# Loading the last second-layer pieces by column halves, and storing left halves of the output behind them

## The chip, the cores and the metric

The kernel runs on one core of a Trainium2 chip. The metric is device time in microseconds (us), median of three runs. The core has a matrix engine (TensorE, PE in the profile), three engines for elementwise work (VectorE, ScalarE, GpSimd: DVE, ACT, POOL) and a sync engine (SyncE, SP) whose queue issues every transfer between main memory and the on-chip memory here. Transfers run on 16 DMA engines. A transfer is cut into packets: one packet for each contiguous run of bytes.

## The reference

An attention over 8 batches, 8 heads, 576 positions gives a matrix `x` of 4608 rows and 512 columns. A soft mixture of experts follows, and only its end matters here:

```python
slot_input = (d.T @ x).reshape(E, S_per_e, D)     # 8 experts, 4 slots each, 512 wide
for e in range(E):
    h = np.maximum(slot_input[e] @ w1[e], 0.0)    # 512 -> 1024
    slot_out[e] = h @ w2[e]                       # 1024 -> 512
...
return (c @ slot_out)                             # 4608 x 32 times 32 x 512
```

`c` is a softmax over the 32 slots of every row's logits. Every row of the output needs all 32 rows of `slot_out`, and a column of the output needs only that column of `slot_out`. All values are 32 bits wide.

## The kernel before

The attention part works through four pairs of batches. While it runs, the weights of the experts are already being loaded: `w1` and `w2` are 16 MB each, and a load moves a piece of 1 MB. A pool of such slots (`ws`) lies over buffers of the attention part as they come free.

**First layer.** For each expert two pieces of `w1` are multiplied with the slot inputs (`expert_in`, L1332); 32 rows by 256 columns leave at a time, four such tiles side by side. A ReLU and a transpose give `hT`, the hidden values with hidden units on partitions.

**Second layer.** `expert_out` (L1366) loads each `w2[e]` in two pieces. A piece holds 512 hidden units as 128 partitions with twice two rows of 512 columns. `mult` makes four matmuls for each column half: the left 256 columns gather in the bank `kvbank`, the right 256 in `scbank` (`pacc[0]` and `pacc[1]`), over all 16 pieces. The sums stand as four stacks of 32 partitions, to be added at the end. The last of the 16 pieces is loaded in four quarter-size transfers, left columns first.

**Weights of the rows.** `slots(bp)` makes `c` for one of four row blocks (`L` holds the logits, 128 partitions with 9 rows each), splits each value into a rounded part and a rest, and transposes it into `cT`.

**The end.** `slot_sums` (L1303) copies each accumulator to `accs` and adds the four stacks with one matmul by the constant `rep` (L1316) into `so`; `sr` holds the sum as a rounded part (L1499) and a rest (L1504). `out_mult` (L1513) makes one row block of 128 by 512 of the output in a bank, from `cT` and `sr`; ACT or DVE copies it to an output buffer (L1566, L1568); three such blocks go to main memory in one transfer of 768 KB (L1576), in runs of 6 KB for each partition. The first three blocks are made in column halves and stored one by one, in runs of 2 KB (L1546).

**What sets the order.** A planner (`Plan.order`) writes the whole order of every engine's instructions ahead, from costs that the code gives for each step and from a model of the DMA engines (`DMA_RATE` and so on). The program then runs each engine's list in order; an instruction waits for what it needs, and what stands behind it waits too. The SP queue is such a list as well. A transfer also waits until the eighth transfer before it has landed, since eight completion semaphores are used in turn.

Of the kernel before, what the change touches and what calls it, by code (L numbers as in the profile page):

```python
# [17 lines left out]
FILL = 10 ** 6  # L18


class Plan:
# [57 lines left out]
    def order(self):  # L79
# [13 lines left out]
        while ready:  # L93
# [44 lines left out]
            if dma:  # L138
                start = max(t, dma_free)
                dma_free = start + dma  # L140
                end[i] = dma_free + self.DMA_LAG
                free[eng] = start
            else:
                end[i] = free[eng] = t + cost
# [124 lines left out]
def kernel(  # L269
# [226 lines left out]
    DMA_RATE = 412e3  # L496
    IN_RATE = 386e3

    def load(dst, src, nbytes, w, pri=None):
        add(  # L500
            SP, 0.06, lambda: nc.sync.dma_start(dst(), src), w=[w],  # L501
            dma=nbytes / (DMA_RATE if nbytes in (1 << 20, 1 << 18) else IN_RATE), pri=pri,
        )
# [738 lines left out]
    NOUT, G = 6, 3  # L1242
# [20 lines left out]
    )  # L1263
    late_tiles = []

    def late(x, off, n):
        if not late_tiles:
# [3 lines left out]
            late_tiles.append(pool.tile([P, J * HALF + JN + DM], F32, name="cS"))  # L1271
        return late_tiles[x][:, off: off + n]

    def after_q(x, off, n, count=1):
# [6 lines left out]
    css, cxs, acs = (  # L1281
        after_q(1, 0, J * HALF), after_q(1, J * HALF, JN), after_q(1, J * HALF + JN, DM)
# [5 lines left out]
    EG = 4  # L1288
    hTb = hTs.tile().split(E // EG)
# [12 lines left out]
    so = [b_l.tile(), b_m.tile()]  # L1302

    def slot_sums():
        for d in range(2):
# [7 lines left out]
            )  # L1313
            add(
# [8 lines left out]
    def expert_in(e, hb):  # L1323
        w1v = w1[e].rearrange("(c p) f -> p c f", p=P)
        w1b = [load_w(w1v[:, 2 * i: 2 * i + 2], wqs if e == EG else ws) for i in range(2)]
        for i in range(2):

            def f(i=i):
                wv = w1b[i].ap.rearrange("p (c f) -> p c f", c=2)
                for c in range(2):  # L1330
                    for j in range(4):
# [3 lines left out]
                            wv[:, c, 256 * j: 256 * j + 256],  # L1335
# [33 lines left out]

    def expert_out(e):  # L1370
        w2v = w2[e].rearrange("(j p t) d -> p j (t d)", j=4, t=2)
        w2h = w2[e].rearrange("(j p t) d -> p j t d", j=4, t=2)
        for i in range(2):
            last = e == E - 1 and i == 1
            t = ws.tile()
            wide = lambda t=t: t.ap.rearrange("p (j t d) -> p j t d", j=2, t=2)

            def mult(dst, d0, n, start, stop, i=i, wide=wide):
                for t in range(2):
                    for j in range(2):  # L1380

                        x = 2 * t + j
                        nc.tensor.matmul(  # L1383
                            dst[NS * x: NS * x + NS, :n],
                            hT()[:, 4 * t + 2 * i + j, NS * e: NS * e + NS],
                            wide()[:, j, t, d0: d0 + n],
                            start=start,
                            stop=stop,
                            tile_position=(0, NS * x),
                        )  # L1390

            if not last:
                load(
                    lambda t=t: t.ap.rearrange("p (a x) -> p a x", a=2),
                    w2v[:, 2 * i: 2 * i + 2], 1 << 20, t,
                )
                for d in range(2):
                    add(
                        PE, (0.5, 16),
                        lambda d=d, mult=mult, i=i: mult(  # L1400
                            pacc[d].ap[:, 0], d * HD, HD, e == 0 and i == 0, False
                        ),
                        r=[hTb.part(e // EG), t], w=[pacc[d]],
                    )
                continue
            t.split(4)
            for d in range(2):
                for j in range(2):
                    load(
                        lambda d=d, j=j: wide()[:, j, :, d * HD: d * HD + HD],  # L1410
                        w2h[:, 2 * i + j, :, d * HD: d * HD + HD], 1 << 18, t.part(2 * d + j),
                    )
            for d in range(2):
                add(
                    PE, (0.5, 16), lambda d=d, mult=mult: mult(pacc[d].ap[:, 0], d * HD, HD, False, True),
                    r=[hTb.part(e // EG), t.part(2 * d), t.part(2 * d + 1)], w=[pacc[d]],
                )

# [3 lines left out]
    cT = {}  # L1422

    def slots(bp):
        Lb = L[bp]
        lv = Lb.ap.rearrange("p (j n) -> p j n", j=J)
        mx, sm, cxb, csb = cmxs.tile(), csms.tile(), cxs.tile(), css.tile()
        cx = lambda: cxb.ap.rearrange("p (j n) -> p j n", n=NS)
# [8 lines left out]
            r=[Lb, mx], w=[cxb],  # L1437
# [9 lines left out]
        add(DVE, 1.2, f, r=[cxb], w=[sm, cxb])  # L1447

# [9 lines left out]
        for t, js in enumerate((range(0, 6, 2), range(6, J, 2))):  # L1458
# [9 lines left out]
            add(PE, len(js) * 0.14, f, r=[csb, ident_b], w=[tp], also=[ct])  # L1468
# [19 lines left out]
    for e in range(E):  # L1488
        expert_out(e)
        if e < NBP:  # L1490
            slots(e)


    slot_sums()
    outv = out.rearrange("(p j) d -> p j d", j=J)
# [26 lines left out]
    ot0 = ots.tile().split(2 * G)  # L1522
    for d in range(2):
        x = slice(d * HD, d * HD + HD)
        for i in range(G):
            po = b_o.tile()
            add(
                PE, 0.22, lambda po=po, i=i, x=x: out_mult(0, i, po, x),
                r=[sr.part(d), cT[0]], w=[po], also=[ot0],
            )  # L1530

            def f(po=po, i=i, d=d):
                dst = ot0.ap[:, i * DM + d * HD: i * DM + d * HD + HD]
                if d == 0 or i == 1:
                    nc.scalar.copy(dst, po.ap[:, :HD])
                else:
                    nc.vector.tensor_copy(dst, po.ap[:, :HD])

            add(
                *((ACT, act(HD)) if d == 0 or i == 1 else (DVE, dve(HD))), f,  # L1540
                r=[po], w=[ot0.part(2 * i + d)],
            )
            if d == 1:
                add(
                    SP, 0.06,
                    lambda i=i: nc.sync.dma_start(  # L1546
# [66 lines left out]
```

## Time and profile before

| | before |
|---|---|
| median of 3 runs | 207.63 us (207.09 to 207.95) |
| profiled execution, its own time | 207.2 us |
| its span, first to last instruction | 205.4 us |
| moved by DMA | 76.47 MB in 28986 packets, 372 GB/s over the span |
| read from main memory, written to it | 66.65 MB, 9.44 MB |
| busy: PE, DVE, POOL, ACT | 82%, 65%, 41%, 34% |

The page of the profile gives busy shares in 40 slices of 5.1 us, the chain of work that ended last, and groups of instructions. Other views give the instructions in order of time, who waited for whom, and, for chosen stretches of the span, the busy time of each engine with the clock that TensorE was granted (1.00 is full), the mean busy share of the 16 DMA engines, and GB/s. That share counts the time of packets, which overlap a little, so that a full stretch reads 1.02 to 1.06.

### The profile page before, as it was taken

To read this page: it belongs to the slowest core of one execution; us is meant where nothing else is said; L and a number is where in the kernel's file an instruction comes from. 1 tells how busy PE (TensorE), PEld (TensorE's weight loads), DVE (VectorE), ACT (ScalarE), POOL (GpSimd) and SP (SyncE) were. 2 spreads that over 40 slices of the span, in tenths; PEclk is the share of its full clock that TensorE was granted. 3 is DMA by queue.
4 is the path that set the end of the run, shared out by engine and by line. 5 is a ranking of instruction groups with operands and counts; after the bars stand their busy time and mean duration, and the time that the engine had idled before them with its cause. 6 is when DMAs were issued, how large, how long until landed. Compare 5 with 4: busy or idle time off the path is not lost.

```text
span 205.4 us, 5935 instructions
## 1 busy us (share of the span) xinstructions
PE 167.9 (82%) x2565; PEld 106.1 (52%) x2565; DVE 133.3 (65%) x232; ACT 69.8 (34%) x183; POOL 84.2 (41%) x84
## 2 busy tenths in 40 slices
PE   7999649978699899788999787989999957989400
PEld 6677534635366586455576364656555523545100
DVE  7822540899897999999899984672558400486500
ACT  2022405446541846436453430200113300475300
POOL 7199205689992995799834482000000000000000
PEclk9999996999979999999999999999999997899755
DMA  6999999999999999999999999999999995099994
GB/s 204 365 393 392 382 388 383 388 385 383 395 384 388 381 391 390 388 394 401 406 400 412 406 413 408 407 409 407 410 405 406 410 395 183 0 396 409 415 420 201
DMA packets 28986, 76.47 MB, mean 372 GB/s; under 512 B 1824, under 2 KB 6944, under 8 KB 28960
## 3 DMA queue, kind: packets, MB, share of 16 engines
q1 hardware_dynamic: 28960, 76.09, 96.9%
q8 instruction: 20, 0.33, 0.7%
q14 instruction: 6, 0.05, 0.1%
HBM read 66.65 MB, written 9.44 MB: 370 GB/s over the span
## 4 chain that ended last, share of the span: by engine, by line
PE 37%; DMA 21%; DVE 14%; POOL 11%; issue 4%; SPq 4%; ACT 2%; POOLq 1%; DVEq 1%; ACTq 0%
DMA arena<-in_moe_w_dram 9%; DMA arena<-in_v_dram 8%; PE bank L1332 7%; PE scbank L812 6%; PE kvbank L703 4%; PE bank L881 4%; SPq L501 4%; DMA out_dram<-arena 4%; POOL arena L847 3%; POOL arena L668 3%; PE bank L1513 3%; POOL arena L647 3%; POOL arena L870 2%; PE bank L1009 2%; DVE arena L605 2%
## 5 line engine op out<-in xcount | busy, mean ns | idle before, releaser
L647 POOL TENSOR_TENSOR arena<-arena 128x1152 f32<-128x1152 f32 x8 | 21.0, 2632 | 17.4 <-ACT arena L640 14.9
L590 DVE STREAM_TRANSPOSE arena<-top 128x1152 f32<-128x1152 f32 x16 | 21.6, 1353 | 8.2 <-DMA top<-in_q_dram 8.2
L703 PE MATMUL kvbank<-arena 64*32 64x128 f32 x1152 | 21.0, 277 | 6.2 <-issue 2.7
L812 PE MATMUL scbank<-arena 64*64 64x288 f32 x256 | 23.7, 447 | 2.3 <-DVE arena L826 2.3
L519 PE MATMUL kvbank<-ones 128*128 128x256 f32 x82 | 23.4, 422 | 2.4 <-ACT arena L727 1.3
L668 POOL TENSOR_TENSOR arena<-arena 128x128 f32<-128x128 f32 (+2 forms) x32 | 23.4, 730 | 3.2 <-ACT arena L656 1.3
L870 POOL TENSOR_TENSOR arena<-arena,ssm 128x576 f32<-128x576 f32 x16 | 18.3, 1151 | 9.6 <-DVE ssm L866 7.9
L703 PEld LDWEIGHTS kvbank<-arena 64*32 64x32 f32 x1152 | 16.5, 107 | 10.8 <-issue 5.6
L847 POOL TENSOR_TENSOR arena<-arena,smx 128x576 f32<-128x576 f32 x16 | 18.4, 1150 | 7.7 <-DVE smx L842 7.7
L881 PE MATMUL bank<-arena 128*128 128x288 f32 x64 | 18.7, 425 | 1.3 <-DVE arena L873 0.8
L605 DVE TENSOR_REDUCE arena<-arena 128x128 f32<-128x1152 f32 x8 | 17.2, 2155 | 3.9 <-DMA arena<-in_phi_dram 3.7
L519 PEld LDWEIGHTS kvbank<-ones 128*128 128x128 f32 x82 | 15.8, 207 | 6.0 <-ACT arena L727 1.7
L1513 PE MATMUL bank<-sr,cT 64*128 64x512 f32 (+1 forms) x78 | 14.7, 425 | 1.7 <-DVE arena L1568 1.3
L826 DVE STREAM_TRANSPOSE arena<-scbank 128x576 f32<-128x576 f32 x16 | 12.3, 766 | 5.6 <-PE scbank L812 5.5
L812 PEld LDWEIGHTS scbank<-arena 64*64 64x64 f32 x256 | 9.9, 141 | 10.2 <-DVE arena L826 3.7
L852 ACT ACTIVATE arena<-arena 128x576 f32<-128x576 f32 x16 | 10.9, 684 | 11.3 <-POOL arena L847 11.1
L881 PEld LDWEIGHTS bank<-arena 128*128 128x128 f32 x64 | 11.2, 189 | 6.4 <-DVE arena L873 2.1
L1383 PE MATMUL kvbank<-arena 128*32 128x256 f32 x128 | 10.8, 411 | 3.8 <-DMA arena<-in_moe_w_dram 3.8
L1568 DVE COPY arena<-bank 128x512 f32<-128x512 f32 x17 | 11.1, 688 | 4.2 <-PE bank L1513 2.5
L873 DVE STREAM_TRANSPOSE arena<-arena 128x576 f32<-128x576 f32 x16 | 11.9, 755 | 1.5 <-POOL arena L870 1.5
L1332 PE MATMUL bank<-arena,SIM 128*32 128x256 f32 x224 | 12.5, 379 | 0.4 <-DVE SIM L1232 0.4
L857 DVE TENSOR_REDUCE ssm<-arena 128x18 f32<-128x576 f32 x16 | 11.8, 738 | 1.0 <-ACT arena L852 0.7
(130 smaller groups left out, 238.4 us busy)
## 6 DMA issues: line engine op xcount, KB each, us to landing
arena<-in_moe_w_dram SPq DMA_DIRECT2D x29, 1024.0 KB, 15.3
top<-in_q_dram SPq DMA_DIRECT2D x8, 1152.0 KB, 12.6
arena<-in_k_dram SPq DMA_DIRECT2D x8, 1152.0 KB, 10.1
arena<-in_v_dram SPq DMA_DIRECT2D x8, 1152.0 KB, 12.5
out_dram<-arena SPq DMA_DIRECT2D x11, 768.0 KB, 8.7
arena<-in_phi_dram SPq DMA_DIRECT2D x8, 576.0 KB, 7.1
top<-in_moe_w_dram SPq DMA_DIRECT2D x2, 1024.0 KB, 11.1
arena<-in_moe_w_dram SPq DMA_DIRECT2D x4, 256.0 KB, 14.6
```

Source lines behind the costliest of these rows:

```text
L519: lambda: nc.tensor.matmul(warm.ap, ones, ones.unsqueeze(1).to_broadcast([P, 2, P]), start=True, stop=True,),
L590: lambda: nc.vector.transpose(qT.ap.rearrange("p (i u y) -> p u i y", i=2, y=Y), qt.ap[:, h * QT_SZ: h * QT_SZ + QT_SZ].rearrange("p (u i ...
L605: lambda: nc.vector.tensor_reduce(mx.ap[:, c0:c1], ph().rearrange("p c j m -> p c m j"), axis=AX.X, op=ALU.max),
L647: lambda: nc.gpsimd.tensor_tensor(ph(), ph(), mb.ap[:, c0:c1].unsqueeze(2).to_broadcast([P, c1 - c0, J, M]), op=ALU.subtract,),
L668: plus = lambda o, x, y: nc.gpsimd.tensor_tensor(o, x, y, op=ALU.add)
L703: nc.tensor.matmul(acc.ap[M * c: M * c + M, a, : 2 * D], ph()[h0: h0 + HALF, c, j, :], kv()[h0: h0 + HALF, :, c, j * D: j * D + D], start= ...
L812: nc.tensor.matmul(scb.ap[HALF * g: HALF * g + HALF, a, :JY], pair[g].kd.ap[h0: h0 + HALF, i, c].rearrange("p r m -> p (r m)"), pair[g].qT ...
L847: lambda: nc.gpsimd.tensor_tensor(exv(), exv(), bc(mx), op=ALU.subtract),
L870: lambda: nc.gpsimd.tensor_tensor(exv(), exv(), bc(sm), op=ALU.mult),
L881: nc.tensor.matmul(lp.ap[:, :JY], vpb.ap[:, h, :], aT.ap[:, a * JY: (a + 1) * JY], start=(h == 0), stop=(h == H - 1),)
L1332: nc.tensor.matmul(hb.ap[NS * j: NS * j + NS, :256], SIM.ap[:, 2 * i + c, NS * e: NS * e + NS], wv[:, c, 256 * j: 256 * j + 256], start=(e ...
L1513: nc.tensor.matmul(po.ap[:, : x.stop - x.start], cT[bp].ap[y: y + HALF, j // 2 * P: j // 2 * P + P], sr.ap[y: y + HALF, t, x], start=(t == 0),
```

## The change

1. The last four pieces of `w2` (both pieces of the last two experts, 4 MB) are no longer loaded whole. First the left 256 columns of all four are loaded, in eight transfers of 256 KB, and then the right 256 columns, in eight more. These have runs of 1 KB, as the four quarters of the last piece had. PE makes the left products of these four pieces first.
2. The other twelve pieces are cut over the partitions in another way: a partition holds four neighbouring rows of `w2[e]`, one run of 8 KB, where it held two runs of 4 KB. The hidden units change places to match, so `expert_in` now reads `w1` with two columns taken and two skipped.
3. Six groups of three row blocks are stored in column halves of 384 KB (runs of 1 KB): the left halves as soon as the left sum is there, the right halves later. The other six groups stay whole. The output buffers are ten instead of six.
4. The left halves of the first three blocks don't go through `rep` and `sr`. `slots(0)` transposes their `c` four times, one copy for each stack (`t4`, copied to `c4`), and `direct` multiplies it with `accs` in one full 32-bit matmul. Each is stored by itself, 128 KB.
5. The transposes of `c` for row blocks 1 to 3 get a late place in the order (`TURN`), `c` is made in place in `L`, and `so[1]` moves to the second half of `kvbank`. Thirteen matmuls on constants (`keep_warm`) may be placed where the planner sees room.
6. The planner takes 350 instead of 412 GB/s for transfers with 1 KB runs, and adds 1 us to the landing of such a load.

```diff
-    NOUT, G = 6, 3
+    NOUT, G = 10, 3
...
                             hb.ap[NS * j: NS * j + NS, :256],
                             SIM.ap[:, 2 * i + c, NS * e: NS * e + NS],
-                            wv[:, c, 256 * j: 256 * j + 256],
+                            wv[:, c, 512 * (j // 2): 512 * (j // 2) + 512].rearrange(
+                                "p (x u t) -> p x u t", u=2, t=2
+                            )[:, :, j % 2, :],
...
     def expert_out(e):
-        w2v = w2[e].rearrange("(j p t) d -> p j (t d)", j=4, t=2)
+        w2v = w2[e].rearrange("(i p x) d -> p i (x d)", i=2, x=4)
         for i in range(2):
             t = ws.tile()
+            if 2 * e + i >= 2 * E - NT:
+                tails.append((e, i, t.split(4)))
+                continue
+            load(
+                lambda t=t: t.ap, w2v[:, i], 1 << 20, t,
+            )
...
+    def tail_out():
+        for d in range(2):
+            for e, i, t in tails:
+                w2h = w2[e].rearrange("(i p j t) d -> p i j t d", i=2, j=2, t=2)
                 for j in range(2):
                     load(
...
+                        w2h[:, i, j, :, d * HD: d * HD + HD], 1 << 18, t.part(2 * d + j),
                     )
+        for d in range(2):
+            for e, i, t in tails:
                 add(
+                    PE, (0.45, 16),
+                    lambda d=d, e=e, i=i, t=t: mult(pacc[d].ap[:, 0], e, i, t, d),
                     r=[hTb.part(e // EG), t.part(2 * d), t.part(2 * d + 1)], w=[pacc[d]],
                 )
+                if (d, e, i) != (1, E - 1, 1):
+                    keep_warm([t.part(2 * d), t.part(2 * d + 1)])
...
+            for i in range(ND):
+                for x in range(0, P, NS):
+                    nc.tensor.matmul(
+                        t4.ap[x: x + NS, i * P: i * P + P], cx()[:, i, :], ident,
+                        start=True, stop=True, tile_position=(0, x),
+                    )
...
+    def direct(i0, i1):
+        for i in range(i0, i1):
+            po, ot = b_o.tile(), half[0]
+            add(
+                PE, 0.45,
+                lambda po=po, i=i: nc.tensor.matmul(
+                    po.ap[:, :HD], c4.ap[:, i * P: i * P + P], accs.ap[:, :HD],
+                    start=True, stop=True,
+                ),
...
+                lambda i=i: nc.sync.dma_start(outv[:P, i, :HD], ot.ap[:, i * DM: i * DM + HD]),
...
     for d in range(2):
         x = slice(d * HD, d * HD + HD)
+        for (bp, j0), ot in zip(groups, half):
+            if (bp, j0, d) == (0, 0, 0):
+                continue
+            for i in range(G):
+                po = b_o.tile()
+                add(
+                    PE, 0.22,
+                    lambda po=po, bp=bp, j=j0 + i, x=x: out_mult(bp, j, po, x),
...
+            store(bp, j0, x, ot, [ot.part(G * d + i) for i in range(G)])
+    for bp, j0 in groups[NA:]:
+        ot = ots.tile().split(G)
...
+        store(bp, j0, slice(0, DM), ot, [ot])
```

On the SP queue, the place is the end of the loads and the stores behind them (`in_moe_w_dram` are the weights, `out_dram` is the output, `arena` the on-chip buffer; the sizes are partitions by elements of one transfer). Before:

```order
L501 DMA arena<-in_moe_w_dram 128x2x1024 x19
L501 DMA arena<-in_moe_w_dram 128x2x256 x4
L1546 DMA out_dram<-arena 128x512 x3
L1576 DMA out_dram<-arena 128x1536 x11
L1608 UNCONDITIONAL_BRANCH
```

And now:

```order
L500 DMA arena<-in_moe_w_dram 128x2x1024 x4
L500 DMA arena<-in_moe_w_dram 128x2048 x12
L500 DMA arena<-in_moe_w_dram 128x2x256 x16
L1567 DMA out_dram<-arena 128x256 x3
L1603 DMA out_dram<-arena 128x3x256 x11
L1603 DMA out_dram<-arena 128x1536 x6
```

Sixteen transfers of 256 KB stand where three whole pieces and four quarters stood, and 20 stores where 14 stood.

On PE, the place is the end of the second layer and the first outputs (`scbank` and `kvbank` with `arena` are the second layer's right and left products, `ident,cS` the transposes of `c`, `cS,rep` the sum over the stacks, `sr,cT` the output blocks). Before:

```order
L1383 MATMUL kvbank<-arena 32x256 x4
L1383 MATMUL scbank<-arena 32x256 x4
L1383 MATMUL kvbank<-arena 32x256 x4
L1383 MATMUL scbank<-arena 32x256 x4
L1316 MATMUL bank_65<-cS,rep 128x256
L1316 MATMUL bank_63<-cS,rep 128x256
L1513 MATMUL bank_62<-sr,cT 128x256 x2
L1513 MATMUL bank_64<-sr,cT 128x256 x2
```

And now:

```order
L1396 MATMUL kvbank<-arena 32x256 x4
L1508 MATMUL bank_64<-ident,cS 128x128 x3
L1508 MATMUL bank_63<-ident,cS 128x128
L1508 MATMUL bank_63<-ident,cS 64x128
L1555 MATMUL bank_62<-cS 128x256
L1396 MATMUL scbank<-arena 32x256 x4
L1320 MATMUL bank_65<-cS,rep 128x256
L1555 MATMUL bank_64<-cS 128x256
L1396 MATMUL scbank<-arena 32x256 x4
L1555 MATMUL bank_63<-cS 128x256
L1591 MATMUL bank_62<-sr,cT 128x256 x2
```

The last left product is the first row; the first `direct` block (L1555) follows it ahead of all four right products of the last pieces, and the left output blocks stand between the right products. The third and the fourth right product come after three and seven of the fifteen left blocks that go through `sr`. Of the thirteen matmuls on constants, one stands between the left and the right blocks and twelve behind PE's last output block.

More of the change, by code (lines that the diff above doesn't have):

```diff
@@ L1263 @@
     )
+    ND = 3
     late_tiles = []
@@ L1313, in slot_sums @@
             )
+            if d == 0:
+                direct(0, 1)
             add(
@@ L1447, in slots, with f @@
         add(DVE, 1.2, f, r=[cxb], w=[sm, cxb])
+        if bp == 0:
+            t4 = b_m.tile()
+            def f():
+                for i in range(ND):
+                    for x in range(0, P, NS):
+                        nc.tensor.matmul(
+                            t4.ap[x: x + NS, i * P: i * P + P], cx()[:, i, :], ident,
+                            start=True, stop=True, tile_position=(0, x),
+                        )
+            add(PE, (0.25 * ND, 16 * ND), f, r=[cxb, ident_b], w=[t4])
+            add(
+                ACT, act(ND * P), lambda: nc.scalar.copy(c4.ap, t4.ap[:, : ND * P]),
+                r=[t4], w=[c4],
+            )
         def f():
@@ L1491, with evict @@
             slots(e)
+    tail_out()
+    groups = [(bp, j0) for bp in range(NBP) for j0 in range(0, J, G)]
+    half = [ots.tile().split(2 * G) for _ in groups[:NA]]
+    def evict(dst, po, n, x):
+        return (ACT, act(n), lambda: nc.scalar.copy(dst(), po.ap[:, :n])) if x else (
+            DVE, dve(n), lambda: nc.vector.tensor_copy(dst(), po.ap[:, :n])
+        )
+    def direct(i0, i1):
+        for i in range(i0, i1):
+            po, ot = b_o.tile(), half[0]
+            add(
+                PE, 0.45,
+                lambda po=po, i=i: nc.tensor.matmul(
+                    po.ap[:, :HD], c4.ap[:, i * P: i * P + P], accs.ap[:, :HD],
+                    start=True, stop=True,
+                ),
+                r=[accs.part(0), c4], w=[po], also=[ot],
+            )
+            add(
+                *evict(lambda i=i: ot.ap[:, i * DM: i * DM + HD], po, HD, i % 2),
+                r=[po], w=[ot.part(i)],
+            )
+            add(
+                SP, 0.06,
+                lambda i=i: nc.sync.dma_start(outv[:P, i, :HD], ot.ap[:, i * DM: i * DM + HD]),
+                r=[ot.part(i)], dma=P * HD * 4 / HALF_RATE,
+            )
+    outv = out.rearrange("(p j) d -> p j d", j=J)
     slot_sums()
-    outv = out.rearrange("(p j) d -> p j d", j=J)
+    direct(1, ND)
     for d in range(2):
```

163 lines of the change are left out of this document (69 added, 94 removed).

## Prediction

> **What bounds the kernel now.** I read the slices of the page first, for where the transfers stop, then short stretches of the span around that place, and then the instructions in order of time there.
>
> ```profile
> DMA  6999999999999999999999999999999995099994
> GB/s 204 365 393 392 382 388 383 388 385 383 395 384 388 381 391 390 388 394 401 406 400 412 406 413 408 407 409 407 410 405 406 410 395 183 0 396 409 415 420 201
> ```
>
> The DMA engines are full from the start to the end, but for one hole in slices 34 and 35. So the time is the time of the bytes plus the hole. The stretches (PE, PEld, DVE, ACT, POOL busy, granted clock, DMA share, GB/s) show it:
>
> ```profile
> 112.00:124.00 12.00, 9.93 (x99) 6.32 (x98) 10.99 (x22) 4.20 (x14) 6.78 (x6) 1.00 1.03 409
> 166.00:170.00 4.00, 1.66 (x32) 0.75 (x32) 0.00 (x0) 0.00 (x0) 0.00 (x0) 1.00 1.04 387
> 170.00:172.00 2.00, 0.57 (x12) 0.08 (x4) 0.00 (x0) 0.00 (x0) 0.00 (x0) 1.00 0.63 229
> 172.00:174.00 2.00, 1.98 (x20) 1.13 (x24) 0.00 (x0) 0.00 (x0) 0.00 (x0) 0.55 0.38 133
> 174.00:176.00 2.00, 2.00 (x17) 0.80 (x10) 0.42 (x1) 0.17 (x1) 0.00 (x0) 0.60 0.02 5
> 176.00:179.50 3.50, 3.45 (x22) 2.29 (x21) 1.70 (x4) 2.24 (x7) 0.00 (x0) 1.00 0.00 0
> 184.00:202.00 18.00, 8.20 (x40) 4.50 (x38) 7.26 (x11) 5.56 (x10) 0.00 (x0) 0.74 1.02 416
> ```
>
> The loads don't end at once: from 170 to 174 the share falls in steps, since some of the 16 engines are through four microseconds before the last. Finer stretches (no instructions, so: clock, share, GB/s) date the ends:
>
> ```profile
> 173.50:174.00 0.50, 0.50 0.20 70
> 174.00:174.50 0.50, 0.50 0.06 21
> 174.50:175.00 0.50, 0.50 0.00 0
> 179.50:180.00 0.50, 1.00 0.45 172
> 180.00:180.50 0.50, 1.00 1.02 377
> 180.50:181.00 0.50, 1.00 1.05 385
> 181.00:181.50 0.50, 1.00 1.03 377
> 202.50:203.00 0.50, 0.50 0.49 197
> 203.00:203.50 0.50, 0.50 0.06 25
> 203.50:204.00 0.50, 0.50 0.06 25
> 204.00:204.50 0.50, 0.50 0.00 0
> ```
>
> A share of 0.06 is one engine of 16. The slowest engine's loads end near 174.4, and the first store's data moves at about 179.78 (0.45 of a full 1.02 in that half microsecond). So the slowest engine stands still for **5.4 us**, the mean engine for longer: the shares missing to full from 170 to 180 add up to 0.4·2 + 0.65·2 + 2 + 3.5 + 0.3, about 7.9 us. The stores end at 202.75 on nearly all engines, and on one at 204.0. What fills the hole is a chain of small steps:
>
> ```profile
> 174.44 1.33 PE L1383 MATMUL scbank<-arena 128*32 128x256 f32 x8
> 174.74 0.42 DVE L1309 COPY cS<-kvbank 128x256 f32<-128x256 f32 x1 [12.69 <-PE kvbank L1383]
> 175.69 1.26 PE L1316 MATMUL bank<-cS,rep 128*128 128x256 f32 x4
> 176.43 0.37 ACT L1499 CAST sr<-bank 128x256 fp32r<-128x256 f32 x1 [0.23 <-PE bank L1316]
> 176.88 3.29 PE L1513 MATMUL bank<-sr,cT 64*128 64x256 f32 x20
> 178.90 1.34 SPq L1546 DMA_DIRECT2D out_dram<-arena  x3
> ```
>
> The last product, the copy, the sum, the rounded part, the first blocks, the first store at 178.90, and 0.9 us later its bytes.
>
> **The change, part by part.** *Whole pieces with 8 KB runs* (12.58 MB). With 4 KB runs loads move 409 GB/s (stretch 112 to 124). No row has 8 KB runs; the nearest is stores with 6 KB at 416 (184 to 202). One end is no gain; the other is a fixed cost for each packet that halves. Stores with 2 KB runs moved 380 (the three rows from 180.0 to 181.5). Over 16 engines a packet of 6 KB at 416 takes 236 ns and one of 2 KB at 380 takes 86 ns: 37.5 ns for each KB and 11 ns fixed. Without half of the fixed part the pieces save 128·12·11/16 ns, about 1.0 us. I take 416 GB/s: 30.8 − 30.2, **−0.5 us** (0 to −1.0).
>
> *Column halves of the loads.* 3.15 MB more than before go in 1 KB runs. The rows of the last quarters have it: 133 GB/s at a share of 0.38 is 350 for all engines, 229 at 0.63 is 363. At 360, 8.75 − 7.70: **+1.05 us** (+0.8 to +1.3).
>
> *Column halves of the stores.* 4.72 MB go in 1 KB runs, where 0.79 MB had 2 KB and 3.93 MB had 6 KB. No row shows a store with 1 KB runs. The fit above gives 48.7 ns for a packet, 336 GB/s. The low bound is the reads' 360; the high bound is that a packet never costs less than the 86 ns of 2 KB, 190 GB/s. I take 336, since a fixed part per packet also fits the reads: 14.05 us against 2.07 + 9.45: **+2.5 us** (+1.6 to +13).
>
> *The hole.* The loads end on the slowest engine at 174.4 − 0.5 + 1.05 = 174.95. The left halves land one stretch of right halves earlier, 2.10 MB at 360 or 5.8 us: at L = 169.1. What follows L, at the full clock:
>
> ```profile
> 121.81 3.17 PE L881 MATMUL bank<-arena 128*128 128x288 f32 x12
> 154.97 0.61 PE L1383 MATMUL kvbank<-arena 128*32 128x256 f32 x8
> 155.40 0.61 PE L1383 MATMUL scbank<-arena 128*32 128x256 f32 x8
> L1537 DVE COPY arena<-bank 128x256 f32<-128x256 f32 x2 | 0.8, 424 | 0.7 <-PE bank L1513 0.6
> L1513 PE MATMUL bank<-sr,cT 64*128 64x512 f32 x66 | 12.7, 442 | 1.7 <-DVE arena L1568 1.3 <-ACT arena L1566 0.4
> ```
>
> A column half of a piece takes 0.43 us on PE (from 154.97 to 155.40). A full 32-bit matmul with 256 columns takes 0.47 (3.17/12 · 256/288, twice). A copy takes 0.42, and each handover about 0.1, as in the chain. So L + 0.5 last left product, + 1.0 copied, + 1.5 first `direct` block, + 2.0 its store issued, + 2.85 its bytes. Before, the same way through `rep` and `sr` took from 174.4 to 179.8. The right pieces then hold PE's list up: a piece's right half lands each 1.45 us, at L + 1.5, 3.0, 4.4 and 5.8, and PE stands in order before each. By the new order the second and the third block leave PE at L + 2.8 and 3.9, the first group of three at 4.6, the next at 5.7, 7.0, 8.0 and 8.6, each 1.5 us later as bytes (copy, issue, start). Behind them PE makes three half blocks in 0.7 us, and a group's 393 KB take 1.17 us of DMA: from there transfers are the limit.
>
> So an engine that ends its loads early waits for these blocks: it is fed without pause from the first full group, 6.1 us after L, at 175.2. Then come 4.33 MB at 336 (12.9) and 4.72 MB at 416 (11.35): 199.45, against 202.75 before, −3.3. The slowest engine has no pause at all: 174.95 + 14.05 + 11.35 = 200.35, **−2.4**. Its own sum is −5.4 − 0.5 + 1.05 + 2.5. The engine that trailed by 1.25 us before is either of the two kinds, so its end falls by 2.4 to 3.3. I take **−2.8 us**.
>
> The SP list costs nothing here: a transfer waits for the eighth before it, and eight of 256 KB are 5.8 us of work, longer than the four microseconds by which the engines differ; without that cover the early engines would stop, which costs them up to the 3.3 − 2.4 that they are ahead. It would be otherwise if small transfers did not overlap. The shortest way from issue to landing was that of a 256 KB store:
>
> ```profile
> DMA to landing us min/median/max: 2.1/4.3/4.4
> ```
>
> Paid by each of the nine more loads and six more stores, that is 31 us, and the kernel would take 239. But the quarters kept the rate of their runs with others in flight: 1 in 100. [...]
>
> The reading of `w1` with two columns taken and two skipped costs nothing if PE reads as fast. PE has this much room:
>
> ```profile
> L1332 PE MATMUL bank<-arena,SIM 128*32 128x256 f32 x224 | 12.5, 379 | 0.4 <-DVE SIM L1232 0.4
> 166.90 0.64 PE L1383 MATMUL kvbank<-arena 128*32 128x256 f32 x8 [0.81 <-DMA arena<-in_moe_w_dram]
> L1464 PE MATMUL bank<-ident,cS 128*128 128x128 f32 x16 | 2.6, 283 | 0.6 <-DVE cS L1453 0.6
> ```
>
> PE waits for a piece for the first time at 166.9, having worked off its backlog at 165.5 to 166; moving three of the four sets of transposes later takes about 2 us off it. The twelve small transposes for `c4` and the copies come ahead and have that room. The moved sets are done between left products, where PE now waits. That may also keep the clock, which fell to half at 172 after PE had been busy for 2.2 of 6 us. With half the clock the blocks come some 1.5 us later, which costs the early engines that much and the slowest nothing: 0 to 0.6 at the end. The constant matmuls stand behind the last block and are hidden by the stores that still run.
>
> Against the profiled execution's own 207.2 us: 204.4. That run lies 0.4 under the median of 207.63, so **204.8 us** as a median.
>
> **The rivals.** *More than that (chance 0.16).* If a read or write of 1 KB costs no more than the reads' low end, the 8 KB runs give 1.0, and the spread of the engines closes so that the mean pause counts, the sum is about −7.9 + 2.0 (pause left) − 1.0 + 0.8 + 1.6 = −4.5: 203.1. The falling steps from 170 to 174 speak against it, since the slow engines carry their delay into the stores.
>
> *The stores are dear (0.10).* A store of 1 KB may cost more than the line through two points says. The gain is gone when the 4.72 MB take 2.8 us more, at 280 GB/s; at 250 they take 18.9, and the time is 207.6 − 2.8 + 4.9 = 209.7, slower. For it: no row has it, and 2 KB already lost 9% against 6 KB. Against: reads of 1 KB hold 350.
>
> *PE comes late (0.09).* If the skipping read of `w1` takes twice as long, the 256 such matmuls (12.5 us for 224) add 14 us. PE has 2.2 of room before L + 0.5: from 165.5 less 2, the four left products and the moved transposes take it to 167.4. The left blocks then come 11.8 us late, the first full group at 187.0, and the end is 187.0 + 12.9 + 11.35 + 1.25, or 212.5 against 204.0: 216. Slower begins at 6.5 us added (2.2, the early engines' 3.3 and the 1.0 that can be told), half more per matmul. No strided read of this kind stands in the trace. [...]
>
> *The left halves don't get ahead (0.12).* PE's list is in order. If right halves land late, or the clock is low, so that the stores are fed two microseconds later than worked out, the slowest engine also pauses, and the change gives 0 to −1: 207.0.
>
> **How the numbers follow.** Forecast 0.52, more 0.16, left halves late 0.12, dear stores 0.10, PE late 0.09, the rule on batches 0.01. The measurement tells about 0.5% from no change, 1.04 us. Faster: 0.52 and 0.16 and a part of the late left halves, less what the forecast's own bounds lose, 0.72. The same 0.15, slower 0.13. The range of the forecast alone is 203.6 to 206.2, from the bounds of its terms. To hold 8 in 10 it reaches into the better rival and over the late left halves: 202.6 to 208.2.
>
> **What would show it.** In the changed profile the share should fall only a little between loads and stores, with the first bytes of the output about 3 us after the last left half. 1 KB stretches of stores should read near 336 GB/s, the 12 whole pieces above 409, the last stores 416. The matmuls of `w1` should keep 379 ns. The forecast is wrong if the stores of column halves lie below 280, if PE reaches its last left product well after the data, or if a hole of more than three microseconds stays on the mean engine.

## The result, and the profile after

| | before | after |
|---|---|---|
| median, four runs each | 207.58 us (207.09 to 207.95) | 205.97 us (205.92 to 206.15) |
| profiled execution, its own time | 207.2 us | 206.0 us |
| its span | 205.4 us | 204.1 us |

The medians differ by 1.6 us. The ratio of the runs is 0.994, with a 95% interval of 0.992 to 0.997, which is 0.6 to 1.7 us: faster. The prediction had 2.8. The direction holds, and by the medians 43% of the amount is missing.

The page of the changed kernel: the slices, and the row of the queue on which the engines' programs are fetched.

```profile
DMA  6999999999999999999999999999999999599993
GB/s 203 368 391 392 382 387 384 386 387 382 395 382 390 384 391 388 384 396 398 406 392 413 409 409 409 414 430 413 425 413 422 372 311 333 198 338 340 412 410 151
...
q8 instruction: 21, 0.34, 0.7%
```

The hole of two slices has become one slice at half. Before, the last row read 20 packets; it will matter. Stretches of the same trace show the loads in long runs, a dip among the short ones from 164 to 166, the rest of the hole, the stores, and the end. The columns are those of the prediction's stretches:

```profile
140.00:155.00 15.00, 15.00 (x268) 8.99 (x260) 10.02 (x30) 2.46 (x6) 0.00 (x0) 1.00 1.01 417
164.00:166.00 2.00, 1.99 (x24) 0.78 (x24) 0.00 (x0) 0.00 (x0) 0.00 (x0) 1.00 0.83 271
166.00:172.50 6.50, 6.37 (x51) 3.12 (x52) 1.76 (x4) 2.40 (x9) 0.00 (x0) 1.00 1.05 341
172.50:177.00 4.50, 4.50 (x44) 2.34 (x42) 2.17 (x6) 1.77 (x5) 0.00 (x0) 1.00 0.49 164
177.00:189.00 12.00, 11.48 (x85) 8.21 (x82) 9.41 (x22) 7.57 (x19) 0.00 (x0) 1.00 1.02 340
...
200.50:201.00 0.50, 0.00 (x0) 0.00 (x0) 0.00 (x0) 0.00 (x0) 0.00 (x0) 0.50 0.58 234
201.00:201.50 0.50, 0.00 (x0) 0.00 (x0) 0.00 (x0) 0.00 (x0) 0.00 (x0) 0.50 0.06 25
...
202.00:202.50 0.50, 0.00 (x0) 0.00 (x0) 0.00 (x0) 0.00 (x0) 0.00 (x0) 0.50 0.09 37
```

Nearly all engines end at 200.8, 1.95 us ahead of the 202.75 of before. One engine (0.06 of 16) goes on to 202.45, so 1.65 us behind the others, where it was 1.25 before. The end of the trailing engine fell by about 1.5 us, close to the 1.6 by which the medians differ.

The chain behind the last left half, in order of time:

```profile
168.72 0.98 PE L1508 MATMUL bank<-ident,cS 128*128 128x128 f32 x7
...
169.63 0.16 PEld L1396 LDWEIGHTS kvbank<-arena 128*32 128x32 f32 x8 [0.20 <-issue]
169.63 0.64 PE L1396 MATMUL kvbank<-arena 128*32 128x256 f32 x8
...
170.34 0.42 DVE L1311 COPY cS<-kvbank 128x256 f32<-128x256 f32 x1 [0.20 <-PE kvbank L1396]
...
170.91 0.67 PE L1555 MATMUL bank<-cS 128*128 128x256 f32 x2
...
172.07 3.16 SPq L1567 DMA_DIRECT2D out_dram<-arena  x3
...
172.61 0.59 PE L1555 MATMUL bank<-cS 128*128 128x256 f32 x2
...
173.14 0.64 PE L1396 MATMUL scbank<-arena 128*32 128x256 f32 x8
...
173.71 0.70 PE L1555 MATMUL bank<-cS 128*128 128x256 f32 x2
...
174.33 0.73 PE L1591 MATMUL bank<-sr,cT 64*128 64x256 f32 x6
...
175.54 1.76 SPq L1603 DMA_DIRECT2D out_dram<-arena  x2
```

The first store is issued at 172.07 and the first full group at 175.54. The DMA engines are full from 177.0, where the prediction had them fed from 175.2. The last left product (169.63) waited for no data: its weight load waited for "issue" alone, behind seven of the moved transposes in PE's list.

### The profile page after: what moved, and what is told of

Its sections match the earlier page's. It is cut to its first block, busy times and chain, and to the rows that moved or that the text cites. A ratio compares the mean times of both kernels' runs of the same rounds, so it can differ in the third digit from the quotient of the medians.

```text
span 204.1 us, 6131 instructions
## 1 busy us (share of the span) xinstructions
PE 176.8 (87%) x2645; PEld 114.5 (56%) x2645; DVE 134.6 (66%) x243; ACT 70.3 (34%) x188; POOL 84.3 (41%) x84
## 4 chain that ended last, share of the span: by engine, by line
PE 38%; DMA 22%; DVE 14%; POOL 11%; issue 4%; SPq 4%; ACT 2%; POOLq 1%; DVEq 0%
DMA arena<-in_moe_w_dram 14%; DMA arena<-in_v_dram 9%; PE bank L1591 6%; PE scbank L811 6%; PE kvbank L702 4%; PE bank L880 4%; SPq L500 4%; POOL arena L846 3%; POOL arena L667 3%; PE scbank L1382 3%; POOL arena L646 3%; POOL arena L869 3%; PE bank L1008 2%; DVE arena L604 2%; DVE arena L825 2%
## 5 line engine op out<-in xcount | busy, mean ns | idle before, releaser
L1547 DVE COPY arena<-bank 128x256 f32<-128x256 f32 (+1 forms) x30 | 14.2, 509 | 5.5 <-PE bank L1591 3.7
L1591 PE MATMUL bank<-sr,cT 64*128 64x256 f32 (+1 forms) x102 | 14.6, 355 | 0.5 <-DVE arena L1547 0.3
L1336 PE MATMUL bank<-arena,SIM 128*32 128x256 f32 x224 | 13.2, 390 | 0.4 <-DVE SIM L1231 0.4
L1591 PEld LDWEIGHTS bank<-sr,cT 64*128 64x128 f32 x102 | 10.1, 185 | 5.6 <-DVE arena L1547 4.4
```

The costliest lines, as they stand in the source:

```text
L1591: nc.tensor.matmul(po.ap[:, : x.stop - x.start], cT[bp].ap[y: y + HALF, j // 2 * P: j // 2 * P + P], sr.ap[y: y + HALF, t, x], start=(t == 0),
```

## The experiments

They compare with the kernel before on the same chip. Its median was 207.18 us beside the first four, 207.09 beside the next four, 207.11 beside the third four and 207.27 beside the last two. The theories' letters are those of the expectations. E, the one that matters, says: an engine's program is fetched in blocks while it runs (the row's 21 packets, 0.34 MB), a fetch occupies one DMA engine, and if that falls into the full stream of stores, this engine ends late and the kernel with it.

### Without the constant matmuls

`no_warm` is the changed kernel with both uses of `keep_warm` taken out.

```diff
-            if 2 * e + i >= 2 * E - NT - 6:
-                keep_warm([t])
...
-                if (d, e, i) != (1, E - 1, 1):
-                    keep_warm([t.part(2 * d), t.part(2 * d + 1)])
```

> The changed kernel without the thirteen matmuls on constants. Theory A: they stand behind PE's last block and one between left and right blocks, so nothing changes but that block: 0.0 to 0.2 us faster; the clock stays at 1.0 over the end of the loads. Rival D (the constants keep the clock up): the clock falls to half near 168 to 172 and the left blocks come later, 0.5 us slower. Rival E (instruction fetches run on one DMA engine, which then ends 1.6 us after the others): the last stretch with a share of 0.06 gets shorter by 0.3 to 0.7 us, and the time with it.

204.07 us, ratio 0.984 (0.982 to 0.987): 1.9 us faster than the changed kernel. The way is E's, but the size is not: E had 0.3 to 0.7. Its end:

```profile
172.50:177.00 4.50, 4.50 (x48) 2.45 (x48) 2.36 (x6) 1.89 (x6) 0.00 (x0) 1.00 0.57 190
177.00:189.00 12.00, 11.30 (x82) 7.81 (x78) 9.63 (x22) 7.57 (x19) 0.00 (x0) 1.00 1.02 340
...
200.50:201.00 0.50, 0.00 (x0) 0.00 (x0) 0.00 (x0) 0.00 (x0) 0.00 (x0) 0.50 0.14 49
201.00:201.50 0.50, 0.00 (x0) 0.00 (x0) 0.00 (x0) 0.00 (x0) 0.00 (x0) 0.50 0.00 0
```

All engines end together at 200.57, 0.2 us from the bulk of the changed kernel; the trailing engine is gone. The clock is 1.00 through the short stores here too, so it was not the constants that kept it up, and D is out. Now the fetches near the end, each from the transfers of one microsecond (packets, MB, share of 16 engines). Before, from 181 to 182:

```profile
q8 instruction: 1, 0.02, 5.8%
```

After, from 174 to 175 and from 195 to 196:

```profile
q8 instruction: 1, 0.02, 5.5%
q8 instruction: 1, 0.02, 5.8%
```

Without the constants, from 174 to 175 and none later (its page counts 20 packets again):

```profile
q8 instruction: 1, 0.02, 6.2%
```

5.8% of 16 microseconds is 0.93 us on one engine. Twelve of the thirteen constants stand behind the last output block, and as work they cost at most the 0.2 us between the two bulks. But they lengthen PE's list past one more block (21 packets against 20), and its fetch at 195 meets full stores. `no_warm_b`, the same once more, is the measure for the runs beside it.

> The changed kernel without the thirteen constant matmuls, once more, as the measure for the two runs beside it: 204.0 +- 0.4 us, 3.1 to 3.5 us below the kernel before, and no trailing engine.

204.25 us, 0.986 (0.984 to 0.989). It is the kernel of `no_warm`, where no engine trails. The time is as expected; the distance to the kernel before, 2.8 us, is 0.3 less than the expected 3.1.

### Moving the fetch alone

If E holds, the fetch can be moved by instructions that do nothing else. `before_late13` puts thirteen small matmuls into the kernel before, where PE waits for the last pieces; `late_count` puts them at the same place into the kernel without constants.

```diff
+                if d0 == 0 and 2 * e + i == 2 * E - 4:
+                    for _ in range(13):
+                        nc.tensor.matmul(warm.ap[:, :2], ones, ones[:, :2], start=True, stop=True)
```

> The kernel before with thirteen matmuls of two columns on constants in the second layer, ahead of the first left product of its thirteenth piece, where PE waits for data; the order of all else is unchanged. Only the fetch that stood at 181 moves. Theory E (it costs its DMA engine a microsecond of stores): it falls into the pause, near 179, no engine trails, and the time falls by 0.9 to 1.3 us against the kernel before. Rival (the trailing engine brings its delay from the loads): it still trails, and the time is within 0.4 us of the kernel before.

205.88 us, ratio 0.994 (0.992 to 0.996): 1.4 us faster than the kernel before, with nothing but work added. The fetch, from 175 to 176, stands alone in the pause, and the end has no trailing engine:

```profile
q8 instruction: 1, 0.02, 5.8%
```

```profile
202.00:202.50 0.50, 0.00 (x0) 0.00 (x0) 0.00 (x0) 0.00 (x0) 0.00 (x0) 0.50 0.98 406
202.50:203.00 0.50, 0.00 (x0) 0.00 (x0) 0.00 (x0) 0.00 (x0) 0.00 (x0) 0.50 0.02 0
```

The bulk ends at 202.5, where it was 202.75 before; nearly the whole gain is the trailing engine. The clock is another way by which more work on PE might have helped. It was 1.00 from 174 to 179.5 here, where it had been 0.60 from 174 to 176 before. But the stores begin at 179.6 against 179.78, so that can be 0.2 us of the gain. The result falls to E: the rival had the engine trail still.

> The changed kernel without its constant matmuls, and with thirteen matmuls of two columns on constants in the second layer instead, ahead of the first left product of the thirteenth piece. PE's list is as long as in the changed kernel, but nothing stands between or behind the output blocks. Theory E: a fetch between 185 and 195, one engine trails by 1.0 to 1.8 us, and the time is 1.2 to 1.9 us above the kernel without constants (204.1 to 204.25), so 205.3 to 206.1. Rival (the constants cost as work at the end): 204.1 to 204.4 us and no trailing engine.

208.57 us (206.60 to 209.38), ratio 1.0055: 4.3 us above the kernel without constants, where 1.2 to 1.9 were expected. The fetch is where E has it, between 193 and 194, and one engine trails by 1.65 us, from 203.85 to 205.5:

```profile
172.50:181.00 8.50, 8.50 (x77) 4.70 (x77) 3.58 (x10) 3.85 (x14) 0.00 (x0) 0.98 0.39 132
203.50:204.00 0.50, 0.00 (x0) 0.00 (x0) 0.00 (x0) 0.00 (x0) 0.00 (x0) 0.50 0.67 270
204.00:204.50 0.50, 0.00 (x0) 0.00 (x0) 0.00 (x0) 0.00 (x0) 0.00 (x0) 0.50 0.06 25
...
205.50:206.00 0.50, 0.00 (x0) 0.00 (x0) 0.00 (x0) 0.00 (x0) 0.00 (x0) 0.50 0.00 0
```

The rest comes from the small matmuls, which weren't small:

```profile
165.16 3.06 PE L1393 MATMUL scbank<-ones 128*128 128x2 f32 x26
...
172.48 0.78 PE L1399 MATMUL kvbank<-arena 128*32 128x256 f32 x8
```

The thirteen stand as 26 records of two columns, 118 ns each, and the last left product starts at 172.48 instead of 169.21 in `no_warm`. Part of that is the clock: it was 0.50 from 169.5 to 172.5 here, and 1.00 in `no_warm`. Seven transposes took 1.76 us at 0.50 (170.80), where seven took 0.98 at 1.00 in the changed kernel (168.72); the share of each was not told apart. The bulk of the stores ends 3.3 us later than in the run without constants (203.85 against 200.57), for 3.3 us of delay. So here a delay of the left blocks cost its own length.

The first two attempts at the same question had the thirteen matmuls at the program's start.

> The kernel before with thirteen matmuls of two columns on constants ahead of PE's first constants; every engine's order of all else is unchanged. They move the place in PE's list at which its instructions are fetched next. Theory E (a fetch of 16 KB on one DMA engine costs that engine about a microsecond, which shows at the end when the stores are at full stream): the fetch that stood at 181 moves into the pause between loads and stores (174 to 179.5), no engine trails at the end, and the time falls by 1.0 to 1.3 us against the kernel before. Rival (the trailing engine comes from something else, such as the uneven end of the loads): one engine still trails by more than a microsecond and the time is within 0.5 us of the kernel before.

> The changed kernel without the thirteen constant matmuls between and behind the output blocks, and with thirteen matmuls of two columns ahead of PE's first constants instead. PE's list is as long as in the changed kernel. Theory E (what the constants cost is a fetch of instructions that falls into the stores): 21 fetches again, one of them between 185 and 195, one engine trails by 1.0 to 1.7 us, and the time is 1.2 to 1.9 us above the kernel without constants. Rival (the constants cost what they do as work on PE at the end, by power, by the clock or by semaphores): no difference to the kernel without constants, within 0.5 us.

213.46 us (209.56 to 215.49; ratio 1.018) and 214.74 us (213.96 to 216.36; ratio 1.037). Both theories missed the totals by 6 to 11 us. What E had said of the end came out: with the fetch between 179 and 180, in a pause, all engines end together (first fence, the kernel before with the thirteen), and with a fetch in the stores, one trails from 210.0 to 211.75 (second, the changed one). That fetch stands between 200 and 201, not between 185 and 195, since everything is later in that run.

```profile
206.00:206.50 0.50, 0.00 (x0) 0.00 (x0) 0.00 (x0) 0.00 (x0) 0.00 (x0) 0.50 0.49 197
206.50:207.00 0.50, 0.00 (x0) 0.00 (x0) 0.00 (x0) 0.00 (x0) 0.00 (x0) 0.50 0.00 0
```

```profile
210.00:210.50 0.50, 0.00 (x0) 0.00 (x0) 0.00 (x0) 0.00 (x0) 0.00 (x0) 0.50 0.08 25
...
211.50:212.00 0.50, 0.00 (x0) 0.00 (x0) 0.00 (x0) 0.00 (x0) 0.00 (x0) 0.50 0.03 12
```

The constants at the start took 5.71 us, and PE then stood waiting for its own list ("issue") in the attention part, 4.5 and 3.3 us in the two largest groups; in the kernel before, the first of these groups waits 2.7 us and the second is not among them. From the first kernel's order of time and its waits:

```profile
1.05 5.71 PE L520 MATMUL kvbank<-ones 128*128 128x2 f32 x26 [1.05 <-DVE ones L452]
```

```profile
PE kvbank L710 <- issue: 4.5, 3, 2.8
PE scbank L819 <- issue: 3.3, 1, 3.3
```

How much of the loss is the one and how much the other is open. The profiled execution of `before_13` took 209.56 us, the fastest of its six, so for most of the 6.4 us by which its median is longer there is no trace.

Over all runs: one engine trails, by about 1.1 to 1.8 us, in the six kernels with a fetch in the stores and no pause after it (before, after, `only_8kb`, `halves_512`, `after_count`, `late_count`), and in none of `no_warm`, `before_late13`, `before_13`, `no_overlap` and `left_first_5`.

### The parts of the change

`only_8kb` puts the 8 KB runs and the reading of `w1` to match into the kernel before; `runs_4kb` takes them out of the changed kernel without constants.

```diff
-        w2v = w2[e].rearrange("(j p t) d -> p j (t d)", j=4, t=2)
+        w2v = w2[e].rearrange("(i p x) d -> p i (x d)", i=2, x=4)
```

> The kernel before with the 8 KB runs of the whole second-layer pieces alone (15 pieces, 15.7 MB), and the reading of the first layer's weights that goes with them. Theory A (the time is bytes by the rate of their runs, plus pauses): in the changed kernel the stretch 140 to 155 moved 417 GB/s where 4 KB runs moved 409, so 15.7 MB take 37.7 instead of 38.5 us: 0.8 us faster, with the pause between loads and stores as long as before. Rival B (the runs give nothing, all of the gain is the filled pause): 0.0.

205.95 us, ratio 0.993 (0.991 to 0.995): −1.2 us, of which 0.1 to 0.2 is a trailing engine of 1.1 instead of 1.25 us. That leaves some 1.0 us for fifteen pieces, or 0.8 for twelve.

> The changed kernel without constant matmuls, and with the twelve whole pieces in runs of 4 KB as before the change; w1 is read by neighbouring columns again. If the 8 KB runs are worth what the stretches say (417 to 420 against 409 GB/s over 12.6 MB, 0.6 to 0.8 us): 204.7 to 205.0 us, loads at 409 GB/s, everything else the same. If the skipping read of w1 costs PE time that shows: not slower, or faster.

205.18 us, ratio 0.990 (0.988 to 0.993): 0.9 us above `no_warm_b`. The loads of the two kernels, first with 8 KB and then with 4 KB:

```profile
140.00:155.00 15.00, 15.00 (x248) 8.24 (x241) 6.03 (x17) 1.66 (x4) 0.00 (x0) 1.00 1.01 418
```

```profile
140.00:155.00 15.00, 15.00 (x270) 8.81 (x265) 9.95 (x30) 3.50 (x9) 0.00 (x0) 1.00 1.03 406
```

The runs of the twelve pieces are worth 0.8 to 0.9 us.

`no_overlap` is the kernel without constants, whose left output blocks wait for the right sum as well; the first `direct` block loses its early place in the list with it.

```diff
-                r=[accs.part(0), c4], w=[po], also=[ot],
+                r=[accs, c4], w=[po], also=[ot],
...
-                    r=[sr.part(d), cT[bp]], w=[po], also=[ot],
+                    r=[sr.part(d), accs, cT[bp]], w=[po], also=[ot],
```

> The changed kernel without the thirteen constant matmuls, and with the left halves' output blocks and direct blocks made to wait for the right sum too: all else stays (column halves of loads and stores, 8 KB runs). It measures what storing left halves behind the loads is worth. By the prediction's sum (hole 5.4 us on the slowest engine, all of it covered): 4 to 5.4 us slower than the kernel without constants, so 208 to 209.5 us. By what the trace of the changed kernel shows (2.4 us of idle left on the mean engine where 7.9 stood): 3 to 5 us. Rival (the hole was not what bounded it, and the gain came from the 8 KB runs and the fetch): within 1 us of the kernel without constants.

207.98 us, ratio 1.0036 (1.002 to 1.005), and the hole is back:

```profile
172.50:179.00 6.50, 5.79 (x38) 2.84 (x38) 1.37 (x4) 1.41 (x5) 0.00 (x0) 1.00 0.10 33
...
174.50:175.00 0.50, 0.50 (x2) 0.12 (x2) 0.00 (x0) 0.00 (x0) 0.00 (x0) 1.00 0.02 6
...
179.00:179.50 0.50, 0.50 (x5) 0.42 (x5) 0.43 (x2) 0.36 (x2) 0.00 (x0) 1.00 0.73 244
```

Storing left halves behind the loads is worth 3.7 us (207.98 − 204.25). This is the middle of what the trace of the changed kernel let expect, and less than the prediction's 5.4. But this hole is not the one of before: the slowest engine's loads end near 174.65 and the first store's data moves at about 179.15, which is 4.5 us, where the kernel before had 5.4.

`halves_512` loads a column half as one transfer of 512 KB, so that the rule on the eighth transfer before covers twice the data (in the changed kernel the SP queue waits 3.7 us for landings by it between 162 and 172).

```diff
-                    1 << 18, t.part(2 * d + j),
+                    1 << 19, t.part(d),
```

The planner's rate and landing time go with the new size.

> The changed kernel with one transfer of 512 KB for a column half of a piece instead of two of 256 KB, so that eight transfers in flight are 4 MB. Runs stay 1 KB. Rival C (early engines run dry at 164 to 166 because the queue waits for the eighth transfer before): the dip to 0.64 to 0.74 of the DMA share goes, and with it 0.4 us. Theory A: the dip goes, but the early engines then finish their loads earlier and stand still for the left blocks instead, so the time stays within 0.2 us.

206.41 us, ratio 0.996 (0.993 to 0.999), against 0.994 of the changed kernel: no gain. (A had the time within 0.2 us; the median is 0.4 longer, and the intervals overlap.) The dip from 164 to 166 gets smaller, and the pause behind it longer:

```profile
164.00:164.50 0.50, 0.44 (x8) 0.29 (x12) 0.00 (x0) 0.00 (x0) 0.00 (x0) 1.00 1.17 358
164.50:165.00 0.50, 0.50 (x12) 0.13 (x4) 0.00 (x0) 0.00 (x0) 0.00 (x0) 1.00 0.71 240
172.00:177.00 5.00, 5.00 (x51) 2.75 (x44) 2.21 (x7) 1.77 (x5) 0.00 (x0) 1.00 0.43 145
```

### Other orders, without the constants

`left_first` puts the left output blocks ahead of the right products in PE's list. `nt5` loads five pieces by halves. `left_first_5` does both, and `left_first_57` stores seven groups by halves besides.

```diff
+    AFTER = (0, 4, 7, 10, 13)     # left_first: (0, 6, 9, 12)
-                    r=[hTb.part(e // EG), t.part(2 * d), t.part(2 * d + 1)], w=[pacc[d]],
+                    r=[hTb.part(e // EG), t.part(2 * d), t.part(2 * d + 1)] + ([tok.part(AFTER[n])] if d else []), w=[pacc[d]],
...
-    NT, NA = 4, 6
+    NT, NA = 5, 6                 # left_first_57: 5, 7
```

> The changed kernel with PE's list put in another order: the left output blocks first, the right products of the last pieces only behind the third direct block and behind left blocks 6, 9 and 12; no constant matmuls. Theory A (the left stores come too late because short PE groups follow each other at 0.57 to 0.63 us each): the first full group of left blocks is issued 1.1 us earlier than 175.5, the pause between 172.5 and 177 shrinks by as much, a new pause of up to 1.4 us may open ahead of the right halves, whose sum comes later; 0.0 to 1.1 us faster than the changed kernel. Rival B (1 KB runs ate the gain): no difference. Rival C (the wait for the eighth transfer before): no difference, and the dip at 164 to 166 stays in both.

204.44 us (204.12 to 206.53), ratio 0.988 (0.983 to 0.993). That is 1.5 us below the changed kernel, but 0.4 above `no_warm`, so no gain of the new order itself is shown. The first full group is issued at 174.61, 0.9 us earlier than in the changed kernel and 0.5 earlier than in `no_warm`, and a new pause stands ahead of the right halves:

```profile
182.00:183.00 1.00, 0.83 (x10) 0.62 (x9) 0.76 (x2) 0.67 (x2) 0.00 (x0) 1.00 0.13 44
```

> The changed kernel without constant matmuls, with the last five pieces by column halves in place of four. The left halves land one more stretch of right halves (1.45 us) ahead of the end of the loads. Theory F (what is left of the pause, 2.5 us on the mean engine between 173 and 177, comes from the left blocks being some 1.2 us later than worked out): the pause falls to 1.0 to 1.5 us, against 0.3 to 0.4 us for two more MB-halves in short runs: 0.5 to 0.9 us faster than four pieces (204.1 to 204.25), so 203.2 to 203.7. Rival (the slowest engine has no pause any more, so only its bytes count): 0.3 us slower than four pieces.

204.26 us, ratio 0.986 (0.983 to 0.988): the same as with four pieces. The pause did fall, to 0.30 · 4.5 or 1.4 us, without a gain; neither theory has both right.

```profile
173.50:178.00 4.50, 4.29 (x51) 2.68 (x44) 2.29 (x7) 2.11 (x7) 0.00 (x0) 1.00 0.70 236
```

> As the run with five pieces, and on PE the left blocks ahead of the right products (right products behind 0, 4, 7, 10 and 13 left blocks). Theory F: stores are fed from about L + 3 without a break, the right halves of the output are what comes late next; 203.0 to 204.0. Rival: what PE's order gives back on the right side (the pause ahead of the right halves, 1.1 us with four pieces) is as long as what it saves on the left: 204.2 +- 0.3.

203.75 us, ratio 0.982 (0.980 to 0.985): the lowest median of all here, 3.4 us below the kernel before and about 2 below the changed one. Its interval still overlaps that of `no_warm` (0.982 to 0.987), so the last 0.3 to 0.5 us are not shown. Loads run into stores without a pause, and the one that is left stands ahead of the right halves:

```profile
172.50:180.50 8.00, 6.97 (x78) 3.87 (x76) 3.76 (x11) 3.12 (x10) 0.00 (x0) 1.00 1.02 350
180.50:182.00 1.50, 1.16 (x12) 0.82 (x10) 1.24 (x4) 1.19 (x4) 0.00 (x0) 1.00 0.14 48
```

> As the run before, and seven groups in column halves in place of six, so that there is 1.2 us more of left stores over the right products. Theory F: no pause ahead of the right halves; 0.8 us saved there against 0.786 MB from 416 to 340 GB/s, 0.42 us: 202.6 to 203.6. Rival (its PE list is longer, a fetch moves into the stores): one engine trails by a microsecond or more, 204.5 or above.

203.80 us, ratio 0.983 (0.981 to 0.986): no different. A pause of 0.55 · 2 or 1.1 us stands from 181 to 183 still, so the seventh group hid little of it and paid its short runs.

## Why the prediction fell short, step by step

**The bound** was right: DMA engines full but for a hole, and the time is the bytes plus the hole.

**The step that failed** is the one on the end of the stores: "The constant matmuls stand behind the last block and are hidden by the stores that still run", and with it the engine that trailed by 1.25 us, which was taken as a property of the engines that the change would carry along. The work is hidden; the fetch that it calls for is not. It was in the profile of before: one packet on the instruction queue at 181 in the stores, one engine late at the end. The matmuls of `before_late13`, which move that packet into the pause, gave back 1.4 us of the kernel before; taking the constants out of the changed kernel gave back 1.7 to 1.9 (1.65 of it the trailing engine). The term stood at 0 and measured +1.7 to +1.9, which is more than the 1.2 us that the result lacks.

**The hole, −5.4,** was too large: the overlap is worth 3.7 us, and with the 0.9 by which the hole of `no_overlap` is shorter than that of before, the term is about −4.6. Those 0.9 come with a granted clock of 1.00 from 172.5 to 179, where it was 0.57 from 172 to 176 before. So the clock did hold, as was hoped of the moved transposes; how much of the 0.9 is the clock is open. Two steps of the way to the feed were late. The last left product starts at 169.63, where L, its data, was put at 169.1. It came late behind the moved transposes, which the prediction had put into PE's waits at no cost. And the first full group is issued 5.9 us behind it, where the prediction had 4.6 to leave PE and one copy more, some 5.2: PE went from one short group to the next in 0.53 to 0.62 us (172.61, 173.14, 173.71, 174.33), instead of the 0.43 to 0.47 that the prediction took from rows of like groups.

**The 8 KB runs, −0.5,** gave 417 GB/s and 0.8 to 0.9 us, near the far end of the range. That the skipping read of `w1` adds nothing was assumed without a run that showed it. It costs PE 390 ns a matmul instead of 379, 3% more, and nobody waits for it:

```profile
L1336 PE MATMUL bank<-arena,SIM 128*32 128x256 f32 x224 | 13.2, 390 | 0.4 <-DVE SIM L1231 0.4
```

The rival of a PE that comes late is out.

**The column halves, +1.05 and +2.5,** were nearly right. Stores move 340 GB/s where 336 was worked out; the rival of dear stores is out. Loads move 341 from 166 on where 360 was taken, 4.19 MB · (1/341 − 1/360) or up to 0.65 us more. What `no_overlap` is above the kernel before, 0.9 us, with the runs' −0.9, the trailing engine's −1.25 and the hole's −0.9 taken off, leaves 3.95 us for the halves, against 3.55. The rates say the same: 3.15 MB at 341 in place of 409 GB/s are 1.5 us, and 4.72 MB of stores at 340 take 2.4 more than the 2.07 + 9.45 of before, together 3.9.

**The SP list "costs nothing here"**: there is a dip of 0.17 · 2 or 0.34 us from 164 to 166. Transfers of twice the size moved that into the pause, so as far as that run shows it cost nothing at the end. The rival of small transfers that don't overlap, with its 239 us ("the rule on batches" among the chances), is out at 205.97.

With these numbers the sum for the kernel without constants is −4.6 − 0.9 + 3.95 − 1.25 = −2.8, against −2.84 and −3.11 measured (3.95 was worked out from the same runs, so the terms add up by construction; only the rates are a check from outside). That this is near the forecast's −2.8 is partly luck: a hole 0.8 us too large and halves 0.4 too small stood against runs 0.4 too small and a trailing engine of 1.25 that vanishes with its fetch.

**The rivals.** "The left halves don't get ahead" had its condition nearly met, a feed 1.8 us late, but its price, a gain of 0 to 1, was not: the kernel without constants has the same late feed and gains 2.8 to 3.1. "More than that" did not come: it needed reads and writes of 1 KB to cost 2.4 us in all, and they cost 3.9. No rival had the instruction fetch in it.

**Open:** a fetch in the stores takes 0.9 to 1.0 us of its engine (5.5 to 6.0% of a microsecond of 16 engines in the six kernels), and the engine trails by about 1.1 to 1.8. The trace doesn't tell what the rest is. Nor does it show on which of the 16 engines a packet ran; that the trailing one is the fetching one is concluded from where fetches and trailing engines stand together.

## What to carry to other kernels

Where a kernel ends on a full stream of transfers, work that is hidden on its own engine is not yet free (here it cost 1.7 to 1.9 us): look at the instruction queue's row of the profile, and at whether a fetch falls into the last stream with no pause behind it; a few instructions less (`no_warm`), or a few more further ahead (`before_late13`), move it (where the engine waits anyway: at the program's start the same thirteen matmuls cost 6 us and more). Where one engine's end trails the others, look for a cause that can be dated before carrying the delay through a sum. And of a hole that is to be covered, price the way from the data to the first full transfer by the handovers between short groups (0.53 to 0.62 us here), not by the pitch inside long ones (0.43 to 0.47).

## What the runs showed of the hardware that was not expected

- One block of a program is 0.34 MB / 21, or 16 KB (the changed kernel's instruction queue), and its fetch took 0.93 us of one DMA engine in a pause (`before_late13`, 5.8% from 175 to 176) and in full stores (the changed kernel, 5.8% from 195 to 196). It is not always so: in the loads of the kernel before it took 1.1 us (6.7%, the packet of 166 to 167), and in `left_first` 1.3 us (8.2%, the packet of 175 to 176).
- A matmul of two columns by a 128 x 128 constant stands as two records in the trace. A record took 118 ns behind the second layer (`late_count`, 3.06 us for 26) and 220 ns at the start (`before_13`, 5.71 us for 26), against 235 ns for 256 columns of the same kind in the changed kernel (6.1 us for 26). So a hundredth of the columns still cost 50% to 94% of the time. In `late_count` the granted clock was 1.00 and the weight loads (PEld) were busy without a gap, 2.50 of 2.50 us from 165.5 to 168; why the start is slower is open.
- Loads in runs of 8 KB moved 417 to 418 GB/s (140 to 155), of 4 KB 406 to 409, of 1 KB 341 (the changed kernel, 166 to 172.5); stores in runs of 1 KB 340 (177 to 189).
